# Two changes to a planned kernel: K of the first chunk placed by ScalarE in layer 1 too, and engine orders drawn up again on a model of the port that VectorE and GpSimd share

## The chip, the cores and the metric

The kernel runs on one core of a Trainium2 chip. The core has five engines that run side by side[...]: TensorE (PE, matmuls; its weight loads are listed as PEld), VectorE (DVE), ScalarE (ACT), GpSimd (POOL) and SyncE (SP, which here only starts DMA transfers). TensorE writes into PSUM, which has eight banks of 512 f32 per partition; the other data lie in SBUF. The metric is the device time of one execution in microseconds, as a median over several executions. Beside it there is one profiled execution, from which every duration below is taken.

## The reference

Two layers with the same weights; each is a windowed attention block and a token-mixing MLP, with layer normalisations and residuals. The input is 2048 tokens of 512 features, bf16; there are 32 heads of 16 features and a window of 256 tokens; the MLP has 1792 hidden units over the token axis.

```python
def _A_ref(x, wqkv, wo):
    H = 32; Dh = D // H; W = 256
    q, k, v = ...                      # x @ wqkv, split in heads
    scores = einsum("bhqd,bhkd->bhqk", q, k) * (Dh ** -0.5)
    mask = (idx[:, None] - idx[None, :] >= 0) & (idx[:, None] - idx[None, :] < W)
    p = softmax(where(mask, scores, -1e9), axis=-1)
    return einsum("bhqk,bhkd->bhqd", p, v)...reshape(B, S, D) @ wo

def _B_ref(x, w1, b1, w2, b2):
    h = layernorm(x)
    u = gelu(einsum("bsd,sf->bdf", h, w1) + b1)
    return (einsum("bdf,fs->bds", u, w2) + b2).transpose(0, 2, 1)

for layer in range(2):
    x = x + _A_ref(layernorm(x), A_wqkv, A_wo)
    x = x + _B_ref(layernorm(x), B_w1, B_b1, B_w2, B_b2)
```

## The kernel before

**Tiling.** The 2048 tokens are four chunks (m = 0 to 3) of four tiles of 128. For each chunk `prepare` normalises the tiles, `qkv` transposes them on TensorE (L750) and projects K, Q (L767) and V (L797); `attention` runs over four groups o of eight heads; `wo_block` projects back and adds the residual (L968, L972); `u_part` adds the chunk's share of the MLP's first matmul to a running sum (L1014, L1023, L1026); `y_block` does the second matmul (L1037, L1042). The y blocks of layer 0 run within layer 1's `prepare`, so that layer 1's attention has MLP matmuls of layer 0 to fill TensorE with, and its own u parts later.

**Attention of one group.** The scores (L851) need K laid out as a block-diagonal `kbd`, in which the even and the odd heads (h = 0, 1) have their own half and zeros elsewhere. ScalarE takes the exponential of two PSUM banks at a time (L863), VectorE multiplies the probabilities `pt` in place by a 0/1 mask from `ldm` (L876 for one cell, L879 for two or more), TensorE multiplies by V (L896), VectorE copies the two results into `cs` (L940), DMAs bring the sums together (L946 to L954 and after) and back as `md` by way of DRAM, and GpSimd multiplies `cs` by `md` into `oT` (L958), which `wo_block` reads.

**How K comes into `kbd`.** The projection leaves K of one group in a PSUM bank. As a rule VectorE (L734) or in some chunks ScalarE (L736) casts it into a bf16 buffer `stg`, and GpSimd writes the two halves of `kbd` from it, each with a 0/1 column of `par` as multiplier (L783). For the groups listed in `KACT`, as (layer, chunk, group), ScalarE writes both halves straight from PSUM with `par` as its scale (L776), and `stg` isn't used. Before, `KACT` holds the four groups of chunk 0 in layer 0.

**Where the order comes from.** Every operation is an entry in a `Graph` with an engine, a cost, the data that it reads and writes, and a priority. `schedule` simulates the five engines: at each step `_pick` chooses for an engine the operation that could start first, with rules for scores, PV matmuls and a priority number; `RANK` shifts the priority of each dense group of matmuls by hand. The outcome is one fixed order of instructions per engine. `reorder` then moves single entries of that order by the offsets in `MOVES` (one tuple each for TensorE, VectorE, ScalarE, GpSimd and SyncE). `emit` writes the instructions out in this order with the semaphore waits that the data need. So each engine runs a fixed list, and an instruction that waits holds up all behind it on its engine, transfers on SyncE's queue included. The costs and simulated times only shape the order; none of them is in the program that runs.

**The port in the planner.** `ported` holds two times, until when VectorE's and until when GpSimd's port operations last. Before, an operation of VectorE counts if it is marked `port` (only the normalisation L700 is), and every operation of GpSimd counts:

```python
            if e == "vector" and o.port:
                t = max(t, self.ported[1])
            elif e == "gpsimd":
                t = max(t, self.ported[0])
...
                if e == "gpsimd" or e == "vector" and o.port:
                    self.ported[e == "gpsimd"] = o.end
```

The masks L876 and L879 are not marked.

Of the kernel before, what the change touches and what calls it, by code (L numbers as in the profile page):

```python
# [21 lines left out]
    -18, 0, -107, -93, 7, 6, -38, -55, -48, 11, -12, 10, 37, -42, 7, 0, -4, -7, 17, -3, -66, 62, -49, 16, 1, 15,  # L22
    -19, 14, -4, 0, 6, 0, -51, 35, 0, 0, 0, 15, -56, -10, 52, 0, -146, 0, -473, -256, 101, -200, 193, 399, 0, 49,
    -23, 0, -1, 18, 8, 17, -12, 11, -1, -10, -4, 7, 6, -31, -47, -15, 10, 0, 0, 15, -362, 42, 322, -14, -380, 0,
    -24, 312, 0, 0, -17, -8, -15, 0, 5, -20, 0, 11, 0, 0, 142, 93, 62, -58, 23, 2, 27, -54, -6, 41, 164, 28, -29,
    -57, 31, 0, 1, -46, 60, 13, 0, -18, 28, -176, 115, -122, 460, -486, -53, 10, -5, 0, 0, 0, 0, 0, -39, -32, -78,
    0, -2, 0, 0, 0, 0, 0, -52, 0, 0, 0, 0, 0, 0, 0, 19, -6, -6, -13, -155, -126, 144, -106, -33, -173, 6, -9, 0,
    -137, 0, 5, -40, 152, 260, 0, -12, 4, 14, -8, 17, -14, 0, 16, -188, 4, 8, 15, -2, 4, -8, 0, 0, -65, 0, 1, 9, -2,
    -112, 11, 0, -15, -114, 0, 7, 3, 4, -12, 10, -16, 0, 9, 6, 12, 0, -28, 0, 0, 117, 31, -17, -17, 0, 0, 473, 47,
    0, -9, -3, -9, -384, -150, -479, 217, 122, 0, 36, 157, 53, 18, -27, 0, -6, 0, -120, 0, 1, 50, 52, 12, 14, 193,  # L30
    -18, 13, 0, 0, 0, 113, 408, -134, 107, -30, -22, -52, 0, 14, -17, 0, 0, 186, -153, -439, 359, -146, 0, -3, 15,
    -10, 13, 10, -109, 5, 157, -86, -10, -52, -43, 17, -46, -58, -33, -135, -167, -266, 232, 53, -3, 56, -33, -31,
    -16, 104, -18, -39, 0, 0, 3, 0, -1, 0, 0, 0, 0, 0, 0, 0, 0, 0, 0, 0, 0, 0, 0, 0, 0, 0, 0, 0, 0, 0, 0, 6,
# [3 lines left out]
        5, 5, -1, 0, 3, 8, -4, 2, -8, 2, -6, 1, -4, 1, -4, 0, 0, 0, 0, 1, 1, -2, 0, 0, 0, 0, 0, 0, 0, 2, -1, -1, 0,  # L37
        0, 0, 0, 0, 0, 0, 0, 1, 3, -2, -1, -1, 0, 0, 1, -1, 0, 0, 0, 0, 0, 0, 0, 1, -1, 0, 0, 0, 0, 0, 0, 0, 0, 0,
        0, 0, 0, 0, 0, 0, 0, 0, 0, 0, 0, 1, -1, 0, 1, -1, 0, 0, 0, 0, 0, 0, 0, 0, 0, 0, 0, 0, 0, 0, 0, 0, 0, 0, 0,
        1, -1, 0, 0, 0, 0, 0, 0, 0, 0, 0, 0, 0, 0, 0, 0, 0, 0, 0, 0, 0, 0, 0, 0, 0, 0, 0, 0, 0, 0, 0, 0, 0, 0, 0, 0,  # L40
        0, 0, 0, 0, 0, 0, 0, 0, 0, 0, 0, 0, 0, 0, 0, 0, 0, 0, 0, 0, 0, 0, 0, 0, 0, 0, 0, 0, 0, 0, 0, 0, 0, 0, 0, 0,
        0, 0, 0, 1, -1, 0, 0, 0, 0, 0, 0, 0, 0, 0, 0, 0, 0, 0, 0, 0, 0, 0, 1, -1, 2, -1, -1, 2, -1, -1, 0, 0, 0, 0,
        0, 0, 0, 0, 0, 0, 0, 0, 0, 0, 0, 0, 0, 0, 0, 0, 0, 0, 0, 0, 0, 0, 0, 0, 0, 6, -1, -1, -1, -1, -1, -1, 0, 1,
        -1, 1, 1, -2, 0, 1, 4, 0, -3, 2, 2, 2, -4, 1, -5, 0, 1, -1, 0, 0, 0, 0, 0, 0, 8, 1, 1, 1, -4, -4, -1, 2, -2,
        -2, 0, 0, 0, 0, 22, 22, 22, -3, -3, 7, 7, 18, 10, 5, 9, 9, 9, -11, -11, -11, -10, -10, -3, -3, -12, -16,
        -13, -6, -14, 1, 1, -16, 0, 0, 0, 0, 0, 0, 0, 0, 0, 0, 0, 0, 0, 0, 0, 0, 0, 0, 0, 0, 0, 0, 0, 0, 0, 0, 0, 0,
        0, 0, 1, -1, 0, 0, 0, 1, 1, -2, 0, 1, -1, 1, 1, -2, 0, 0, 0, 0, 0, 0, 0, 0, 0, 0, 0, 0, 0, 0, 0, 0, 0, 0, 0,
        0, 0, 0, 0, 0, 0, 0, 0, 0, 0, 0, 0, 0, 0, 0, 0, 0, 0, 0, 0, 0, 0, 0, 0, 0, 1, -1, 0, 0, 0, 0, 0, 0, 0, 0, 0,
        0, 0, 1, -1, 0, 0, 3, -1, 0, -2, 0, 4, -1, -1, -1, -1, 3, -1, -1, -1, 0, 0, 0, 0, 0, 0, 0, 0, 0, 0, 0, 0, 0,
        0, 0, 0, 0, 0, 0, 0, 0, 0, 0, 0, 0, 1, -1, 0, 0, 0, 0, 0, 0, 0, 0, 0, 0, 0, 0, 0, 0, 0, 1, -1, 0, 1, -1, 1,  # L50
        -1, 0, 0, 0, 0, 0, 0, 0, 0, 0, 0, 0, 0, 0, 0, 0, 1, -1, 0, 0, 0, 0, 0, 0, 1, -1, 0, 0, 0, 0, 0, 0, 0, 0, 0,
        0, 0, 0, 0, 0, 0, 0, 0, 0, 0, 0, 0, 0, 0, 0, 0, 0, 0, 0, 0, 0, 2, 0, 1, -3, 0, 0, 0, 0, 0, 0, 0, 0, 0, 0, 0,
        0, 0, 1, -1, 0, 0, 0, 0, 0, 0, 0, 0, 0, 0, 0, 0, 0, 0, 0, 0, 0, 0, 0, 0, 0, 0, 0, 0, 0, 0, 0, 0, 0, 0, 0, 0,
        1, -1, 0, 1, -1, 2, -1, -1, 1, -1, 0, 0, 1, -1, 0, 0, 2, 2, 2, -3, 2, -4, -1, 0, 0, 0, 1, 1, 1, 1, -4, 0, 0,
        2, 2, 2, -3, 1, -4, 0, 0, 0, 0, 0, 0, 0, 0, 0, 3, -1, 2, 2, -3, -3, 21, -1, 3, 14, 18, 1, 1, -6, 1, -7, 3,
        14, -9, 1, -4, -7, 13, -2, -2, -15, -9, -9, -4, 3, 9, 5, 5, -8, -5, 8, 4, -11, -5, -9, 11, 3, -4, 4, 4, -11,
        6, -6, -3, 6, -1, -5, 1, -3, 5, 5, -14, 6, -2, -2, -6, 0, 5, 5, -6, -3, 3, 4, -4, -4, 0, 4, 4, -7, -2, 2, 7,
        2, 0, -6, 0, 0, 0, -9, 0, 0, 0,
    ),
    (  # L60
        6, -1, 3, 8, 8, 8, 8, 9, 7, 9, 9, 6, 8, 8, -7, -7, 6, 6, 11, -10, 5, -17, 15, 3, 3, 9, -16, 22, 5, -1, 5,
        -7, -31, -2, 2, 18, 12, 13, -8, -37, 1, -3, -3, 0, -4, 2, -4, 24, -4, -3, 4, -19, -1, 13, 1, -3, 9, 1, -13,
        -3, 4, 2, -5, -1, 16, -5, 9, 1, -1, 0, 2, 2, 2, 8, 2, -16, -15, 5, 9, 6, 4, 2, 4, 5, 5, 5, 5, 6, 4, 5, 5, 5,
        -22, -15, 4, 5, 1, 4, 5, 5, -1, 5, 3, 5, 3, 4, -4, -30, -29, 1, 2, 0, 1, 2, 0, 1, 1, 3, 0, 3, 3, 0, 2, 2, 2,
        2, 2, 2, -9, 1, 1, 1, 1, 1, 1, 1, 1, 1, 2, 0, 1, 1, 3, 1, 2, 3, 1, 2, 3, -6, 0, 2, 2, 2, -2, 4, 0, 1, -1, 2,
        0, 1, 1, 3, 1, 2, 2, 8, 1, -5, 2, 3, 5, -2, 4, 1, 3, 7, -5, -9, 3, 1, -1, 2, -4, 2, 3, -1, 2, 2, -2, 1, 1,
        1, -191, 0, 0, 0, 0, 0, 0, 0, 0, 1, -1, 0, 0, 2, -1, 1, 1, -3, 0, 0, 0, 0, 1, -1, 0, 0, 0, 1, -1, 0, 0, 0,
        0, 2, 0, 2, 0, 2, -5, -1, 1, 1, 2, 2, -1, 2, 0, 2, 0, 1, 1, 2, 6, 2, 0, -15, 1, -1, 2, 3, -1, -9, 2, 0, 2,
        0, -5, 1, -1, 1, 1, 1, 2, -4, -1, 1, 2, 0, 1, 1, -5, 0, 0, 3, 0, 0, -3, 0, 0, 0, 0, 1, -1, 0, 0, 0, 0, 0, 0,
        1, 1, 3, 1, 2, 2, 2, 2, -8, 2, 2, 2, 2, -10, 1, 1, 1, -7, 0, 0, 0, 2, 0, 2, 0, -4, 0, 0, 1, 1, -2, 1, -1, 1,  # L70
        -1, 0, 0, 0, 0, 0, 4, -1, -1, -1, -1, 0, 0, 2, 0, 5, 3, 0, 0, -6, 3, 3, 0, 2, -8, 1, 1, -6, 0, 0, 0, 0, 3,
        1, -1, -3, 5, 1, 2, -3, -1, -4, 0, 0, 0, 0, 0, 0, 0, 0, 0, 0, 1, -1, 0, 0, 0, 0, 1, 1, 1, 1, -4, 0, 0, 0, 0,
        0, 2, 2, 2, 6, -4, 1, -1, 6, 7, -1, 0, -4, -1, -12, 2, 2, -4, 1, 1, -5, 0, 0, 0, 2, -1, -1, 0, 2, 2, 2, -2,
        2, 2, 3, -2, 4, 2, 3, -11, 4, 1, 1, 4, 4, 1, -10, -2, 2, 2, 2, 2, -14, 1, 2, 2, 4, -2, 0, -10, 4, -2, 4, 2,
        4, 2, 3, 3, -7, -7, 2, 2, 3, 3, 0, 2, -5, 3, 0, 2, -1, 1, -19, 0, 0, 3, 0, 0, -3, 0, 1, -1, 0, 0, 4, 1, 3,
        4, -3, 1, 2, -4, 1, 1, 1, 1, 1, 1, 1, 1, 1, 1, -18, 4, -1, 1, -1, 1, -4, 1, 2, -2, 1, 3, 1, 2, 2, -3, 2, 0,
        3, 1, 3, 1, 3, 3, 3, 8, 6, -3, 10, -10, 12, -2, -4, 1, 11, 4, -5, 7, 9, -30, 9, -11, -2, 5, 7, -2, 0, 3, 6,
        3, -13, -10, 4, 2, -1, -19, -21, 0, 0, 0, 1, 1, 1, 1, 1, 1, 1, 1, -8, 0, 0, 0, 0, 0, 0, 0, 0, 0, 0, 2, 0,
        -2, 0, 1, -1, 0, 0, 1, 1, 1, 1, 1, 1, 1, 3, 0, 2, 3, 4, 0, 3, 0, 2, 2, -17, -9, 1, 2, 0, -3, 2, -1, 1, 1, 2,
        2, -1, -6, 1, 1, 1, -3, 0, 1, -1, 0, 1, 1, -2, 0, 1, 1, 2, 4, 2, -5, -1, 1, -5, 1, -1, 2, 0, 1, 4, 1, -5, 3,  # L80
        3, -4, -1, 2, -5, 1, 1, -3, 3, 0, 2, -1, 1, 2, 3, 5, 5, 5, -4, 4, 4, 4, 4, 4, -8, 3, 3, 3, -10, -10, 1, -23,
        0, 0, 0, 3, 0, -2, 1, 4, -3, 0, 0, 1, 2, 3, 1, -7, 3, 5, 8, -1, 4, -4, -2, -10, -1, 2, 4, -6, 1, 2, -5, -3,
        0, 1, 2, -2, -1, 1, -1, 0, 0, 0, 2, 0, -2, 1, 2, -2, -1, 1, 1, 1, -3, 3, -1, 0, -2, 2, 0, -2, 0,
    ),
    (
        0, 0, 0, 0, 1, -1, 0, 0, 0, 1, -1, 0, 0, 0, 0, 0, 0, 0, 0, 0, 0, 0, 0, 0, 0, 0, 0, 0, 0, 0, 0, 0, 0, 0, 0,
        0, 0, 0, 0, 0, 0, 0, 0, 0, 0, 0, 0, 0, 0, 0, 0, 0, 0, 0, 0, 0, 0, 0, 0, 0, 1, -1, 0, 0, 0, 0, 0, 1, -1, 0,
        0, 0, 0, 0, 0, 0, 0, 0, 0, 0, 0, 0, 0, 0, 0, 1, -1, 0, 0, 0, 0, 0, 0, 0, 0, 0, 0, 0, 0, 0, 1, -1, 0, 0, 0,
# [35 lines left out]
KACT = {(0, 0, o) for o in range(4)}  # L124
# [31 lines left out]
class Graph:  # L156
# [108 lines left out]
    def _pick(self, e, cand, ready, free, mode):  # L265
# [8 lines left out]
        for o in cand:  # L274
            t = free
# [5 lines left out]
            elif e == "gpsimd":  # L281
                t = max(t, self.ported[0])
# [831 lines left out]
```

## Time and profile before

| | |
|---|---|
| median of 5 runs | 482.51 us (480.79 to 485.57) |
| profiled execution, its own time | 483.6 us |
| its span, first to last instruction | 481.9 us |
| mean granted TensorE clock | 0.996 |

Groups of instructions that the change concerns, from the profile:

| line, engine | what | count | mean of one |
|---|---|---|---|
| L863 ACT | exponential, 2 banks | 288 | 1037 ns |
| L734 DVE | cast of K to `stg` | 24 | 679 ns |
| L736 ACT | cast of K to `stg` | 4 | 595 ns |
| L783 POOL | half of `kbd` from `stg` | 56 | 779 ns |
| L879 DVE | mask, 1024 elements | 72 | 755 ns |
| L876 DVE | mask, 512 elements | 72 | 498 ns |
| L958 POOL | `oT` = `cs` x `md` | 30 | 1366 ns |
| L696 POOL | power of the normalisation, 2 columns | 24 | 764 ns |

Read the views so: busy time tells how long an engine worked, not whether anyone waited for it. The chain of work that ended last is followed back from the last instruction, at each step to what released it, so an instruction on it did set the end in this execution. A timeline line gives start, duration, engine, source line, operation, operands and count; in brackets stands the idle time before it and what ended that. Neighbouring VectorE instructions overlap a little in the record: a cast listed with 0.68 us is followed by the next after 0.60.

### The profile page before, as it was taken

Reading aid. Unit: us, or ns where it says so; the run is one execution under the profiler, and the core shown is the slowest. Engines: PE = TensorE matmul, PEld = TensorE weight load, DVE = VectorE, ACT = ScalarE, POOL = GpSimd, SP = SyncE. Lnnn points to the kernel's source line nnn. Section 1 sums busy time; section 2 is a strip of 40 time slices with the busy share of each in tenths; the row PEclk is TensorE's granted clock in tenths of the full one; section 3 lists DMA queues with packets and bytes.
Section 4 is the critical chain, followed back from the end, with each engine's and each line's share of the span. In section 5 each row is a group of like instructions: output and inputs, shape, how many; then the busy total and the mean of one; then the engine's idle time right before and its main releaser. Section 6 shows DMA issues by size and latency. Waiting matters only on the chain.

```text
span 481.9 us, 15719 instructions
## 1 busy us (share of the span) xinstructions
PE 436.8 (91%) x6831; PEld 208.7 (43%) x6831; DVE 370.2 (77%) x747; ACT 323.5 (67%) x367; POOL 133.6 (28%) x205
## 2 busy tenths in 40 slices
PE   7988887797888789999999989997989989999997
PEld 4454443353333344455344444443534434444443
DVE  6989989787988979765797698789995986942332
ACT  2889999998988970623898889787868982052000
POOL 3243442343414313025012532443184121200000
PEclk9989999999999999999999999999999999999999
DMA  8403431224153333231044333120415356434564
GB/s 237 146 1 97 113 107 32 57 79 116 41 162 88 109 118 111 66 104 51 12 127 119 92 101 92 53 70 28 121 32 147 100 159 185 119 89 122 164 177 160
DMA packets 83993, 49.47 MB, mean 103 GB/s; under 512 B 14676, under 2 KB 78164, under 8 KB 83924
## 3 DMA queue, kind: packets, MB, share of 16 engines
q1 hardware_dynamic: 83924, 48.46, 35.3%
q8 instruction: 54, 0.88, 0.8%
q14 instruction: 15, 0.12, 0.1%
HBM read 41.43 MB, written 2.59 MB: 91 GB/s over the span
## 4 chain that ended last, share of the span: by engine, by line
PE 60%; DVE 17%; ACT 16%; POOL 3%; issue 2%; DMA 1%; SPq 1%; POOLq 0%
PE PS L1037 17%; PE PS L1014 16%; ACT pt L863 14%; PE PS L767 6%; PE PS L851 5%; PE PS L797 5%; PE PS L896 5%; PE PS L968 3%; DVE pt L876 3%; DVE cs L940 2%; DVE pt L879 2%; POOL kbd L783 2%; DVE qT L734 1%; DVE stats L689 1%; PE PS L616 1%
## 5 line engine op out<-in xcount | busy, mean ns | idle before, releaser
L863 ACT ACTIVATE pt<-PS 128x1024 bf16<-128x1024 f32 (+1 forms) x304 | 284.3, 1026 | 42.9 <-PE PS L851 39.9
L1014 PE MATMUL PS<-xh_sb,w1b 128*128 128x512 bf16 x448 | 106.2, 380 | 3.6 <-ACT pt L863 1.8
L1037 PE MATMUL PS<-ub,w2b 128*128 128x512 bf16 x448 | 103.3, 380 | 0.1
L851 PE MATMUL PS<-qT,kbd 32*128 32x64 bf16 (+4 forms) x1632 | 61.1, 244 | 21.9 <-ACT pt L863 7.4
L767 PE MATMUL PS<-xhT,wqkv 128*128 128x512 bf16 x256 | 63.8, 384 | 1.9 <-ACT pt L863 1.4
L958 POOL TENSOR_TENSOR oT<-cs,md 128x512 bf16<-128x512 f32 x30 | 40.9, 1366 | 87.5 <-DMA cs<-cs 47.4
L1014 PEld LDWEIGHTS PS<-xh_sb,w1b 128*128 128x128 bf16 x448 | 40.1, 98 | 57.0 <-issue 5.7
L1037 PEld LDWEIGHTS PS<-ub,w2b 128*128 128x128 bf16 x448 | 41.5, 98 | 50.6 <-issue 3.7
L783 POOL TENSOR_SCALAR kbd<-stg,par 128x512 bf16<-128x512 bf16 x56 | 43.2, 779 | 60.7 <-DVE stg L734 37.7
L879 DVE TENSOR_TENSOR pt<-pt,ldm 128x1024 bf16<-128x1024 bf16 (+1 forms) x80 | 56.9, 721 | 3.2 <-ACT pt L863 3.1
L1026 DVE TENSOR_TENSOR ub<-PS,ub 128x512 f32<-128x512 f32 x70 | 45.3, 684 | 15.6 <-PE PS L1014 15.4
L851 PEld LDWEIGHTS PS<-qT,kbd 32*128 32x128 bf16 x1632 | 23.5, 92 | 75.3 <-ACT pt L863 40.4
L1042 DVE SCALAR_TENSOR_TENSOR x_sb<-PS,bcol,x_sb 128x512 bf16<-128x512 f32 x32 | 23.4, 746 | 41.6 <-PE PS L1037 41.5
L940 DVE COPY cs<-PS 128x512 f32<-128x512 f32 x60 | 38.6, 683 | 14.1 <-PE PS L896 13.8
L1029 ACT ACTIVATE ub<-ub,bcol 128x512 bf16<-128x512 f32 x28 | 18.3, 712 | 43.7 <-DVE ub L1026 43.6
L876 DVE TENSOR_TENSOR pt<-pt,ldm 128x512 bf16<-128x512 bf16 (+1 forms) x104 | 43.6, 440 | 2.2 <-ACT pt L863 1.8
L896 PE MATMUL PS<-pt,vt 64*18 64x64 bf16 (+4 forms) x3040 | 39.0, 242 | 6.4 <-DVE pt L876 1.8
L694 POOL TENSOR_SCALAR rstd<-agg 128x2 f32<-128x2 f32 (+1 forms) x40 | 8.9, 222 | 125.4 <-DVE agg L691 124.3
L689 DVE BATCH_NORM_STATS2 stats<-x_sb 128x6 f32<-128x512 bf16 x64 | 42.7, 681 | 0.9 <-DMA x_sb<-in_A_x_dram 0.6
L896 PEld LDWEIGHTS PS<-pt,vt 64*18 64x18 bf16 x3040 | 30.7, 84 | 15.8 <-ACT pt L863 3.6
L797 PE MATMUL PS<-wqkv,xhT 128*64 128x256 bf16 x512 | 33.7, 277 | 2.3 <-DVE cs L940 0.8
L767 PEld LDWEIGHTS PS<-xhT,wqkv 128*128 128x128 bf16 x256 | 22.1, 98 | 30.2 <-issue 3.2
(54 smaller groups left out, 324.8 us busy)
## 6 DMA issues: line engine op xcount, KB each, us to landing
w2b<-in_B_w_dram SPq DMA_DIRECT2D x112, 128.0 KB, 2.6
w1b<-in_B_w_dram SPq DMA_DIRECT2D x56, 256.0 KB, 3.4
md<-rscr SPq DMA_DIRECT2D x30, 256.0 KB
cs<-cs SPq DMA_DIRECT2D x120, 32.0 KB, 2.9
out_dram<-x_sb SPq DMA_DIRECT2D x16, 128.0 KB, 3.0
x_sb<-in_A_x_dram SPq DMA_DIRECT2D x3, 512.0 KB
wqkv<-in_A_wqkv_dram SPq DMA_DIRECT2D x2, 384.0 KB, 7.5
x_sb<-in_A_x_dram SPq DMA_DIRECT2D x4, 128.0 KB, 2.1
```

The source lines that it names most:

```text
L689: op("vector", lambda e, t=t: e.bn_stats(stats[:, t, :], x_sb[:, t, :]), reads=[f"x{t}"], writes=[f"st{t}"], cost=dve_cost(512))
L767: mm_group(ft, 4, lambda e, c: e.matmul(PS[:, ft.slot, :], lhsT=wqkv[:, c, which * 512 + o * P:which * 512 + (o + 1) * P], rhs=xhT[:, tx.s ...
L783: op("gpsimd", lambda e, h=h: e.tensor_scalar(kbd[:, tk[o].slot, :, h, :], stg[:, ts.slot, :].rearrange("p (s n) -> p s n", n=64), par[:, ...
L797: last = e.matmul(PS[64 * hf:64 * hf + 64, ft.slot, sc * 256:(sc + 1) * 256], lhsT=xhT[:, tx.slot, c, tok:tok + 64], rhs=wqkv[:, c, 1024:1 ...
L851: last = e.matmul(PS[:, bank(r), c0 * 64:(c0 + nb) * 64], lhsT=kbd[32 * r:32 * r + 32, tkk.slot, jj, :, :].rearrange("p h n -> p (h n)"), ...
L863: return e.activation(pt[:, tp.slot, 2 * u:2 * u + 2, 0:n], PS[:, b0:b0 + 2, 0:n], ACTF.Exp, scale=SMSCALE)
L876: return e.tensor_tensor(v, v, msk.unsqueeze(1).to_broadcast([P, 4, w]), op=ALU.mult)
L879: return e.tensor_tensor(v, v, msk.unsqueeze(1).unsqueeze(1).to_broadcast([P, 4, k, w]), op=ALU.mult)
L896: last = e.matmul(PS[32 * r:32 * r + 18, tO[h].slot, q0 * 64:(q0 + nb) * 64], lhsT=vt[64 * h:64 * h + 64, tvv.slot, jj, 4 * o + r, :], rhs ...
L940: op("vector", lambda e, tO=tO[h], tc=tc, h=h: e.tensor_copy(cs[:, tc.slot, h], PS[:, tO.slot, :]), reads=[tO[h]], writes=[(tc, h)], cost= ...
L1014: out_ = e.matmul(PS[:, tu.slot, :], lhsT=w1b[:, tw.slot, s, tt * P:(tt + 1) * P], rhs=xh_sb[:, 4 * m + s, :], start=(n == 0 and s == 0), ...
L1037: mm_group(ft, NFT, lambda e, fc: e.matmul(PS[:, ft.slot, :], lhsT=w2b[:, tws[fc // W2F].slot, fc % W2F, k * P:(k + 1) * P], rhs=uT(fc), s ...
```

## The change

`KACT` takes in chunk 0 of layer 1. In the planner, masks are marked `port`, and so are the long GpSimd operations (L783, the V placements L813, L958); GpSimd's other operations, the two of each normalisation (L694, L696) among them, no longer count. Two windows of `_pick` for layer 0 are 250 and 50 ns in place of 300 and 0. `RANK` and all five tuples of `MOVES` are new: the order of every engine is another. Of the instructions that run, only those for K of chunk 0 in layer 1 are of another kind.

```diff
 RANK = (
...
 MOVES = (
...
-KACT = {(0, 0, o) for o in range(4)}
+KACT = {(l, 0, o) for o in range(4) for l in range(2)}
...
-            if e == "vector" and o.port:
-                t = max(t, self.ported[1])
-            elif e == "gpsimd":
-                t = max(t, self.ported[0])
+            if o.port:
+                t = max(t, self.ported[e == "vector"])
...
-    WINDOW = ({0: 400.0, 1: 300.0, 2: 0.0}, {0: 150.0, 1: 400.0, 2: 400.0})
+    WINDOW = ({0: 400.0, 1: 250.0, 2: 50.0}, {0: 150.0, 1: 400.0, 2: 400.0})
...
-                if e == "gpsimd" or e == "vector" and o.port:
+                if o.port:
                     self.ported[e == "gpsimd"] = o.end
...
-                       reads=[ts, ("par", h)], writes=[(tk[o], h)], cost=pool_cost(512, 1))
+                       reads=[ts, ("par", h)], writes=[(tk[o], h)], cost=pool_cost(512, 1), port=True)
...
-                           writes=[("vb", v0, h)], cost=pool_cost(128, 1))
+                           writes=[("vb", v0, h)], cost=pool_cost(128, 1), port=True)
...
-                        op("vector", f_mask, reads=keys + LD, writes=keys, cost=dve_cost(4 * len(cells) * w, 0.5), tag="mask")
+                        op("vector", f_mask, reads=keys + LD, writes=keys, cost=dve_cost(4 * len(cells) * w, 0.5), tag="mask",
+                           port=True)
...
-                   reads=[(tc, 0), tm] + [(tc, "up", r) for r in range(4)], writes=[to], cost=1400)
+                   reads=[(tc, 0), tm] + [(tc, "up", r) for r in range(4)], writes=[to], cost=1400, port=True)
```

## The prediction

> **What bounds the kernel now.** I read the page's busy row first, then the busy time by stage, then the chain of work that ended last, then the timelines of single engines where the chain pointed. The page, in which each entry is busy time, share of the span and instructions:
>
> ```profile
> span 481.9 us, 15719 instructions
> ...
> PE 436.8 (91%) x6831; PEld 208.7 (43%) x6831; DVE 370.2 (77%) x747; ACT 323.5 (67%) x367; POOL 133.6 (28%) x205
> ```
>
> TensorE is busy in all but 45.1 us (481.9 - 436.8). The change adds and removes no matmul, so what it gains or loses has to appear in those 45.1 us. The stages show where they lie (stretch, its length, then busy time and instructions of each engine):
>
> ```profile
> core 0: us, PE busy (x) PEld busy (x) DVE busy (x) ACT busy (x) POOL busy (x), PEclk, DMA share, GB/s
> 0.00:20.00 20.00, 17.15 (x139) 8.98 (x140) 14.85 (x46) 9.67 (x15) 7.51 (x27) 1.00 0.69 205
> 20.00:180.00 160.00, 135.64 (x2963) 66.47 (x2961) 140.10 (x286) 143.96 (x160) 54.23 (x70) 0.99 0.31 88
> 180.00:244.00 64.00, 63.41 (x489) 29.15 (x491) 46.86 (x95) 28.15 (x37) 13.88 (x27) 1.00 0.25 72
> 244.00:400.00 156.00, 142.19 (x2884) 69.12 (x2880) 130.90 (x260) 130.62 (x142) 53.79 (x72) 1.00 0.35 97
> 400.00:481.90 81.90, 78.44 (x381) 35.01 (x368) 37.45 (x63) 11.08 (x16) 4.16 (x9) 1.00 0.48 142
> ```
>
> TensorE idles 24.4 us in the attention of layer 0 (20 to 180), 13.8 us in that of layer 1 (244 to 400), and next to nothing from 180 to 244, where matmuls of the MLP fill every gap. So 38.2 us can be won, all in the two attention stages. There ScalarE is at 90% and 84%, VectorE at 88% and 84%: three engines pass the limit to and fro. The chain agrees: 60% TensorE, 17% VectorE, 16% ScalarE, 3% GpSimd. Its pieces (start, length, what) include masks far longer than their work:
>
> ```profile
> 280.17 1.60 DVE pt L879
> ...
> 300.00 3.76 POOL kbd L783 x4
> ...
> 396.66 1.35 DVE pt L876
> ```
>
> The L879 mask of 1024 elements usually takes 0.68 us, the L876 mask of 512 takes 0.41. GpSimd's timeline shows what ran beside two of these, and VectorE's timeline shows the same two masks:
>
> ```profile
> 279.95 2.94 POOL L958 TENSOR_TENSOR oT<-cs,md 128x512 bf16<-128x512 f32 x2 [3.34 <-issue]
> ...
> 396.45 1.26 POOL L958 TENSOR_TENSOR oT<-cs,md 128x512 bf16<-128x512 f32 x1
> ```
>
> ```profile
> 280.09 1.68 DVE L879 TENSOR_TENSOR pt<-pt,ldm 128x1024 bf16<-128x1024 bf16 x1
> ...
> 396.58 1.42 DVE L876 TENSOR_TENSOR pt<-pt,ldm 128x512 bf16<-128x512 bf16 x1
> ```
>
> The mask at 396.58 starts 0.13 us behind a GpSimd multiply that ends at 397.71 and itself ends at 398.00, some 0.3 behind it: it stood still for about 1.0 us. This is the collision that the new planner knows of and the old one did not.
>
> **Part 1: K of chunk 0 in layer 1.** It removes four casts to `stg` and eight GpSimd placements, and adds eight ScalarE placements. Layer 0 has these already, so their price is in the trace:
>
> ```profile
> L776 ACT ACTIVATE kbd<-PS,par 128x512 bf16<-128x512 f32 x8 | 5.2, 717 | 0.0
> ```
>
> On the chain a pair of them takes 1.16 to 1.24 us; four pairs are 4.6 us of ScalarE. Removed are 4 x 0.60 = 2.4 us of VectorE (the pace of its casts) and 8 x 0.69 = 5.5 us of GpSimd; the stage in which they lie has 17 us of VectorE idle and most of GpSimd, so I value both at nothing. A placed K would be ready sooner: now the first cast starts at 220.81 and its first halves are placed from 221.61, some 2.2 us for a pair; then 1.2. Whether that starts the exponentials sooner depends on TensorE's order. TensorE, then ScalarE, at this place:
>
> ```profile
> 219.75 5.34 PE L767 MATMUL PS<-xhT,wqkv 128*128 128x512 bf16 x24
> 225.02 0.40 PE L851 MATMUL PS<-qT,kbd 32*128 32x320 bf16 x8
> ```
>
> ```profile
> 217.62 0.59 ACT L736 CAST vt<-PS 128x512 bf16<-128x512 f32 x1
> 225.47 1.94 ACT L863 ACTIVATE pt<-PS 128x1024 bf16<-128x1024 f32 x2 [7.26 <-PE PS L851]
> ```
>
> Six projections run in a row before the first score, and ScalarE waits 7.26 us for it. With a new order the first K is projected at 220.8, placed at 222.1, and the first exponential could start near 222.8, 2.7 us sooner. One pair lies in the 7.26 us for nothing; the other three (3.5 us) stand among the exponentials, and whatever is queued behind them on ScalarE waits, with the scores that need those PSUM banks behind that. Ends: 2.7 us won (the three pairs lie in ScalarE's waits, which from 225.5 to 241.4 sum to 2.4 us) and 4.6 us lost (first score no sooner, every pair in the way). I take 3.5 - 2.7 = 0.8 us lost. The cover that could make it nothing is that TensorE has MLP matmuls to run until 244.
>
> **Part 2: the new orders.** All five engines' orders change, SyncE's too, so no single move can be priced. The trace does show what the model change is aimed at. I went through the chain and took from each collided piece its usual duration:
> - starts that a DMA set, because the GpSimd multiply had waited for `cs` or `md`: masks at 143.00 (0.42), 144.95 (1.07), 174.18 (0.90), 260.42 (0.59), 325.32 (1.05), 327.78 (0.77): 4.8 us;
> - starts that the order set: 124.42 (placements and the power behind them, 0.69), 257.60 (0.38), 280.09 (1.00), 300.00 (four placements at 0.94 in place of 0.67: 1.07), 353.57 (0.82), 396.58 (1.00): 5.0 us.
>
> In all 9.8 us of the chain. Off the chain is as much again: L879 72 x (755 - 682) = 5.3 us, L876 72 x (498 - 411) = 6.3 us, and GpSimd's own, 56 x (779 - 696) + 30 x (1366 - 1273) = 7.4 us, 19 us in all. An order can keep a mask from a placement that is queued by hand, but where a transfer's landing starts the multiply, a plan that mistakes the landing by half a microsecond is no help. So I take the second group, 5.0 us, and leave the first. Ends: 9.8 us won (both groups) and, since the reordering also moves transfers past each other on SyncE and could put anything late, about as much lost as one more long wait costs; the nearest row is ScalarE's waits for scores (39.9 us in 55 waits, 0.7 each), so a handful, 3 us, lost.
>
> Behind a mask that is no longer late stands the next input of the same PV matmul or score: ScalarE's exponentials, 14% of the chain. With ScalarE at 84 to 90% in these stages, more than about half of the chain's collisions cannot be cashed without meeting it; that too is why I stop at 5.0.
>
> One rule speaks against the new model. It counts only GpSimd's long operations as users of the shared port; the small ones of the layernorm (L694, L696) are freed. The rows: L696 takes 0.69 us for two columns as a rule, but 1.23 at 127.48 while a mask ran from 127.48 to 128.17, and 1.17 at 317.52. The Trainium skill, "SBUF — State Buffer", section "SBUF: two separate sides", says that the port pair is an exclusive lock which the first to start keeps for its whole instruction, and that it counts against any GpSimd operation that reads SBUF. By the rule each of the 40 small ones may stop a mask for 0.69 us; by the rows they are those that stop, by 0.5, and the normalisation behind them waits (3.4 us over 5 waits in this profile). By the model they cost nothing. If four more of them lay behind masks on the chain, that would be 2 us lost; I take none, as the old orders did not avoid them either.
>
> **Sum.** 0.8 - 5.0 = -4.2 us. The profiled execution took 483.6 us (span 481.9 and 1.7 around it), 1.1 above the median of 482.51; it would become 479.4, and the median 478.3, 0.9% less.
>
> **Rivals.**
> - *Nothing is won.* The masks are freed, but the exponentials behind them are just as late, and new collisions replace old ones, since the multiplies start when transfers land. For it: six of the twelve places are of that kind, and ScalarE's share. Against it: VectorE itself holds 17% of the chain. Time: 482.5.
> - *ScalarE becomes the bound in layer 1: slower.* The four pairs lie in front of exponentials, and the first score comes no sooner. Price 4.6 us, in full where ScalarE has less than 3.5 us of waits between 225 and 244 and TensorE's filler ends before ScalarE has caught up. For it: those waits are 2.4 us up to 241. Against it: from 244 to 400 ScalarE idles 25.4 us, so that most can be made up. Time: 487.1.
> - *More is won.* Both groups go and the exponentials start 2.7 us sooner: 482.5 - 12.5 = 470.0.
>
> **How the numbers follow.** Forecast 0.53, nothing won 0.20, ScalarE bound 0.15, more won 0.12. Half a percent, 2.4 us, is about what a measurement of this kernel can tell from no change. Faster by over that: 0.65; within it: 0.20; slower by over it: 0.15. The forecast's own range is 475 to 480. The range for 8 in 10 runs from 471.5, most of the way to the best case, to 485.5, inside the ScalarE case.
>
> **What would show it.** TensorE's busy time stays at 436 to 438 while its idle time falls from 45 to about 41 us, the fall lying in 244 to 400 more than in 20 to 180. The 1024 mask's mean falls from 755 to below 720 ns, the 512 mask's from 498 to below 460. Sixteen ScalarE placements at 717 ns; GpSimd placements down from 56 to 48. First exponential of layer 1 about 2.7 us sooner against its stage's first score. It is wrong if the masks' means fall and the span doesn't (nothing won), or if ScalarE has no gap from 222 to 250 and scores wait on it more than now (slower).

## The result and the profile after

| | before | after |
|---|---|---|
| median | 482.82 us (79 runs) | 480.66 us (44 runs) |
| ratio | | 0.9956, 95% interval 0.9942 to 0.9971 |
| profiled execution, span | 481.9 us | 478.6 us |

The changed kernel is 0.44% faster (2.1 us). The forecast was 0.9% (4.2 us): the right way, half the size. The profiled executions differ by 3.3 us, more than the medians; single executions of one kernel differ by a few microseconds, so the sizes below come from the ratios and the profiles tell only where. The changed kernel's line numbers are three smaller (L879 is now L876, L876 is L873, L783 is L780, L776 is L773, L863 is L860).

The page of the changed kernel, and its chain by engine:

```profile
span 478.6 us, 15704 instructions
...
PE 435.9 (91%) x6830; PEld 207.4 (43%) x6830; DVE 366.6 (77%) x746; ACT 326.8 (68%) x372; POOL 127.1 (27%) x197
...
PE 61%; ACT 22%; DVE 8%; issue 3%; DMA 2%; SPq 2%; POOL 2%; POOLq 0%
```

TensorE's busy time stays, as it had to; its idle time falls from 45.1 to 42.7 us. VectorE's share of the chain falls from 17% to 8%, ScalarE's rises from 16% to 22%: ScalarE is now more often the one that is late. The same stages as before (the number in brackets behind each engine's busy time is instructions):

```profile
20.00:180.00 160.00, 136.37 (x2963) 65.91 (x2964) 139.84 (x287) 143.04 (x159) 55.14 (x75) 0.99 0.31 84
180.00:244.00 64.00, 63.45 (x571) 30.06 (x570) 44.77 (x96) 35.20 (x47) 7.96 (x21) 1.00 0.27 78
244.00:400.00 156.00, 145.19 (x2816) 69.16 (x2812) 129.97 (x260) 129.55 (x140) 54.06 (x71) 1.00 0.36 100
```

Between 180 and 244 ScalarE has 7 us more and GpSimd 6 less, and TensorE is as full as it was. TensorE's idle time falls where the forecast put it: from 13.8 to 10.8 us between 244 and 400, and only from 24.4 to 23.6 between 20 and 180. The masks, by form (count, then busy time and mean of one):

```profile
L876 DVE TENSOR_TENSOR pt<-pt,ldm 128x1024 bf16<-128x1024 bf16 x72 | 53.3, 756 | 1.3 <-ACT pt L860 1.2
L873 DVE TENSOR_TENSOR pt<-pt,ldm 128x512 bf16<-128x512 bf16 x72 | 31.6, 451 | 2.0 <-ACT pt L860 1.9
```

The 512 mask's mean fell from 498 to 451 ns, as forecast; the 1024 mask's, which was to fall below 720, did not move (755 before). Collided masks are still on the chain:

```profile
97.48 1.66 DVE pt L876
...
100.88 0.36 DVE pt L873
...
106.80 2.10 DVE pt L876 x2
...
359.60 2.28 DVE pt L876 x2
```

GpSimd's timeline shows the same partner as before at all four. Three of these multiplies were started by a transfer; only the first stood behind other work of GpSimd:

```profile
97.32 1.27 POOL L956 TENSOR_TENSOR oT<-cs,md 128x512 bf16<-128x512 f32 x1
...
100.52 1.27 POOL L956 TENSOR_TENSOR oT<-cs,md 128x512 bf16<-128x512 f32 x1 [0.22 <-DMA md<-rscr]
...
106.49 1.27 POOL L956 TENSOR_TENSOR oT<-cs,md 128x512 bf16<-128x512 f32 x1 [2.33 <-DMA md<-rscr]
...
360.00 1.33 POOL L956 TENSOR_TENSOR oT<-cs,md 128x512 bf16<-128x512 f32 x1 [3.86 <-DMA md<-rscr]
```

Last, K of chunk 0 in layer 1, TensorE and then ScalarE:

```profile
217.70 4.48 PE L764 MATMUL PS<-xhT,wqkv 128*128 128x512 bf16 x20
222.11 0.40 PE L848 MATMUL PS<-qT,kbd 32*128 32x320 bf16 x8
```

```profile
218.77 1.27 ACT L773 ACTIVATE kbd<-PS,par 128x512 bf16<-128x512 f32 x2 [2.23 <-PE PS L764]
220.49 1.27 ACT L773 ACTIVATE kbd<-PS,par 128x512 bf16<-128x512 f32 x2 [0.46 <-PE PS L764]
222.22 1.26 ACT L773 ACTIVATE kbd<-PS,par 128x512 bf16<-128x512 f32 x2 [0.46 <-PE PS L764]
223.37 1.94 ACT L860 ACTIVATE pt<-PS 128x1024 bf16<-128x1024 f32 x2
```

Five projections now run ahead of the first score, not six: the score starts 4.41 us behind the first projection (before: 5.27), 0.9 us sooner. Three pairs, not one, lie ahead of the first exponential. So that exponential starts 5.67 us behind the first projection, where it started 5.72 behind it before: the 2.7 us that I counted did not come.

**A measure of collisions.** For each mask and each normalisation (L700) I took its duration less the lower quartile of its form, wherever that was over 0.12 us, and called the sum of one profile VectorE's collision sum. It is 13.6 us before and 9.4 after. In before's profile 9.9 us of it stand beside the multiply, 3.4 beside placements of K and 0.3 beside a normalisation's power; after, 7.6 and 1.8 and none.

### The profile page after: what moved, and what is told of

It is laid out like the page before. It is cut to its first block, busy times and chain, and to the rows that moved or that the text cites. A ratio compares the mean times of both kernels' runs of the same rounds, so it can differ in the third digit from the quotient of the medians.

```text
span 478.6 us, 15704 instructions
## 1 busy us (share of the span) xinstructions
PE 435.9 (91%) x6830; PEld 207.4 (43%) x6830; DVE 366.6 (77%) x746; ACT 326.8 (68%) x372; POOL 127.1 (27%) x197
## 4 chain that ended last, share of the span: by engine, by line
PE 61%; ACT 22%; DVE 8%; issue 3%; DMA 2%; SPq 2%; POOL 2%; POOLq 0%
ACT pt L860 20%; PE PS L1035 17%; PE PS L1012 16%; PE PS L894 6%; PE PS L764 5%; PE PS L848 5%; PE PS L966 5%; PE PS L794 4%; DVE pt L876 2%; DVE cs L938 2%; DMA w1b<-in_B_w_dram 1%; ACT kbd L773 1%; SPq L992 1%; PE PS L613 1%; SPq L944 1%
## 5 line engine op out<-in xcount | busy, mean ns | idle before, releaser
L860 ACT ACTIVATE pt<-PS 128x1024 bf16<-128x1024 f32 (+1 forms) x304 | 283.8, 1028 | 35.7 <-PE PS L848 33.3
L1012 PE MATMUL PS<-xh_sb,w1b 128*128 128x512 bf16 x448 | 107.6, 382 | 3.9 <-DMA w1b<-in_B_w_dram 1.1
L764 PE MATMUL PS<-xhT,wqkv 128*128 128x512 bf16 x256 | 62.4, 381 | 1.5 <-DVE vt L731 0.9
L956 POOL TENSOR_TENSOR oT<-cs,md 128x512 bf16<-128x512 f32 x30 | 38.8, 1294 | 90.4 <-DMA cs<-cs 46.9
L876 DVE TENSOR_TENSOR pt<-pt,ldm 128x1024 bf16<-128x1024 bf16 (+1 forms) x80 | 56.6, 721 | 3.0 <-ACT pt L860 2.8
L780 POOL TENSOR_SCALAR kbd<-stg,par 128x512 bf16<-128x512 bf16 x48 | 38.0, 801 | 64.2 <-DVE stg L731 49.7
L873 DVE TENSOR_TENSOR pt<-pt,ldm 128x512 bf16<-128x512 bf16 (+1 forms) x104 | 39.2, 399 | 4.0 <-ACT pt L860 3.9
```

What stands on the lines that cost most here:

```text
L764: mm_group(ft, 4, lambda e, c: e.matmul(PS[:, ft.slot, :], lhsT=wqkv[:, c, which * 512 + o * P:which * 512 + (o + 1) * P], rhs=xhT[:, tx.s ...
L860: return e.activation(pt[:, tp.slot, 2 * u:2 * u + 2, 0:n], PS[:, b0:b0 + 2, 0:n], ACTF.Exp, scale=SMSCALE)
L873: return e.tensor_tensor(v, v, msk.unsqueeze(1).to_broadcast([P, 4, w]), op=ALU.mult)
L876: return e.tensor_tensor(v, v, msk.unsqueeze(1).unsqueeze(1).to_broadcast([P, 4, k, w]), op=ALU.mult)
L1012: out_ = e.matmul(PS[:, tu.slot, :], lhsT=w1b[:, tw.slot, s, tt * P:(tt + 1) * P], rhs=xh_sb[:, 4 * m + s, :], start=(n == 0 and s == 0), ...
```

## The experiments

For orders to be moved from one kernel to the other, the program was written again with every engine's order and every tile's buffer as lists: with before's lists it issues before's instructions in before's order, and with the new lists those of the changed kernel. Line numbers of these files are again others.

### What each part does alone, and each layer

```diff
 # k_alone: before's lists
-vector:  ... kc3 kc0 ... kc2 kc1 ...        (four casts)
-gpsimd:  ... kb30 kb00 kb31 kb01 kb21 kb10 kb11 kb20 ...
+scalar:  xhT xhT vt  kb30 kb31 kb00 kb01 kb20 kb21  exp exp vt  kb10 kb11  exp ...
 # orders_alone: the changed kernel's lists
-scalar:  ... the eight kb ...
+vector:  ... kc0 q kc3 q kc2 vt kc1 ...
+gpsimd:  ... kb00 kb01 kb30 kb31 kb20 kb21 kb10 kb11 ...
 # layer0_new: operations of layer 0 as in the new lists, of layer 1 as in the old; layer1_new: the reverse
```

> The kernel before, every engine in its old order, with K of chunk 0 in layer 1 placed by ScalarE: the four casts and eight GpSimd placements are taken out of their queues, and the eight ScalarE placements put in where the changed kernel has them (three pairs ahead of the first two exponentials, one pair behind them). My theory (the new orders win, by fewer masks that meet GpSimd; K is about neutral): 482.8 to 483.6 us, ratio 1.000 to 1.002. Rival 'K does it': 480.7 us, ratio 0.9956. Rival 'ScalarE bound in layer 1': 485 to 487.

> The changed kernel's orders with the K edit taken back: chunk 0 of layer 1 again has four VectorE casts and eight GpSimd placements, put in at the places where K's matmuls end; all else in the new order. My theory: the gain is the orders', 480.7 us or a little less, ratio 0.994 to 0.996. Rival 'K does it': 482.8 us, ratio 1.000.

> Layer 0's operations in the changed kernel's order, layer 1's in the old one, K as before. By the two profiles layer 0 ends 2.05 us sooner after the change (the run of 42 y matmuls starts at 201.88, before at 203.93): if that shift is carried to the end, 480.7 us, ratio 0.9955 to 0.996. By my prediction's view (most of the fall in layer 1): ratio 0.998. If layer 1 gives it back: 1.000.

> Layer 0's operations in the old order, layer 1's in the changed kernel's, K on ScalarE in both layers. By the two profiles 1.2 us of the 3.3 us lie behind 244 us: 481.6 us, ratio 0.997 to 0.998. By my prediction's view: ratio 0.994 to 0.996. If layer 1's new order wins nothing: 1.000.

Measured: k_alone 1.0081 (1.0042 to 1.0119), orders_alone 0.9939 (0.9918 to 0.9961), layer0_new 1.0117 (1.0079 to 1.0156), layer1_new 1.0078 (1.0046 to 1.0110).

The orders win alone what the change wins, so "K does it" falls. K alone cost 3.9 us (486.7), which my theory did not have. The rival "ScalarE bound" did (485 to 487), though not for its reason, as k_early below shows. TensorE's timeline of k_alone:

```profile
226.99 0.81 PE L620 MATMUL PS<-xhT,wqkv 128*128 128x512 bf16 x3 [2.05 <-ACT kbd L629]
```

The fourth pair stood on ScalarE behind two exponentials and a cast; until it had read its PSUM bank, a projection of TensorE that needed the bank waited 2.05 us, and everything behind it on TensorE too. The clock then cost as much again. Three stretches of 3.41 us around this place, the wait lying in the second (PEclk, third from the end, is the granted clock):

```profile
core 0: us, PE busy (x) PEld busy (x) DVE busy (x) ACT busy (x) POOL busy (x), PEclk, DMA share, GB/s
221.22:224.63 3.41, 3.41 (x46) 2.23 (x45) 0.53 (x1) 2.71 (x4) 0.00 (x0) 1.00 0.00 0
224.63:228.04 3.41, 1.36 (x21) 0.57 (x18) 0.89 (x2) 2.08 (x4) 0.00 (x0) 1.00 0.00 0
228.04:231.45 3.41, 3.41 (x18) 1.04 (x8) 1.18 (x2) 1.94 (x2) 0.00 (x0) 0.50 0.02 5
```

By my estimate 3.41 us at half the clock lose 1.7 us of TensorE's work; with the wait that makes 3.75 of the 3.9 us. In the other executions the clock is lower too: its mean is 0.9921 over k_alone's eight and 0.9965 over those of before measured beside them.

The two hybrids were meant to place the gain and didn't. Either half of the new orders beside the other half of the old is slower than both kernels. Their profiles show longer waits for single transfers than TensorE and VectorE have in before's or the changed kernel's profile, such as this of TensorE in layer0_new from 280 to 335:

```profile
PE PS L897 <- DMA w2b<-in_B_w_dram: 4.9, 1, 4.9
```

In layer1_new VectorE waits 4.5 us for the transfer of sums into `rr` between 300 and 320 (before: 0.8 us in the whole profile). Whether the seam between the lists makes these waits was not settled. One thing they did teach: ScalarE's load of a new function table, which follows its last activation of layer 0, starts at 206.43 in before's profile and at 205.39 in the changed kernel's, but at 204.09 and 203.07 in k_alone and layer1_new, which run layer 0 in the old order. (Before's profile has a stretch of 3.4 us at half the granted clock at 29 us; those two have none by then.) The "2.05 us sooner" on which I put layer0_new's number was a difference between two executions, not between two orders.

### Where K may stand

```diff
 # k_early, against k_alone
-scalar:  kb30 kb31 kb00 kb01 kb20 kb21  exp exp vt  kb10 kb11
+scalar:  kb30 kb31 kb00 kb01 kb20 kb21  kb10 kb11  exp exp vt
 # k_pe, against k_alone
-tensor:  K3 K0 Q1 Q0 K2 K1 score V V V V Q3 score Q2
+tensor:  K0 Q1 K3 Q0 K2 score V V V V Q2 K1 Q3 score
-scalar:  kb30 kb31 kb00 kb01 kb20 kb21  exp exp vt  kb10 kb11
+scalar:  kb00 kb01 kb31 kb30 kb21 kb20  exp exp  kb11 kb10  vt
```

> As k_alone (old orders, K of chunk 0 in layer 1 on ScalarE), with the fourth pair of placements also ahead of the first two exponentials. In k_alone TensorE waited 2.05 us at this place for a bank that ScalarE had not yet read, and its clock was halved for 3.4 us afterwards. If the wait is the cause: 483 to 484, ratio 1.000 to 1.003 (1.2 us more of ScalarE ahead of the exponentials remains). If ScalarE's extra 4.6 us are the cause in themselves: no better than k_alone, ratio 1.007 or more.

> As k_alone, with the 14 groups of matmuls at this place (K, Q and V of chunk 0, the first two scores) and ScalarE's placements in the changed kernel's order: the fourth K is projected behind V. If K's cost is set by the order around it: ratio 1.000 to 1.002. If it is ScalarE's load: 1.007.

Measured: k_early 1.0004 (0.9978 to 1.0030), k_pe 1.0122 (1.0075 to 1.0169). With all four pairs ahead of the exponentials K costs nothing that can be told, and the projection that waited in k_alone runs without a wait. The new order of this place, set among old neighbours, is the worst of the three: TensorE waits for ScalarE's placements twice. TensorE's lines, k_early's first, then k_pe's:

```profile
226.26 1.04 PE L620 MATMUL PS<-xhT,wqkv 128*128 128x512 bf16 x4
```

```profile
224.83 1.94 PE L655 MATMUL PS<-wqkv,xhT 128*64 128x256 bf16 x32 [1.03 <-ACT kbd L628]
...
229.96 1.04 PE L619 MATMUL PS<-xhT,wqkv 128*128 128x512 bf16 x4 [1.36 <-ACT kbd L628]
```

All three kernels give ScalarE the same work, so it is not ScalarE's load that costs but the order, by way of the bank. (In k_pe the two waits are 2.4 of 5.9 us; what makes the rest was not followed.) My expectation for k_pe was wrong in taking the new kernel's order of 14 groups to be good by itself.

### What the collisions are worth

```diff
 # np_before, np_after
-gpsimd: kbd half = stg * par;  vb = vt * half;  oT = cs * md
+gpsimd: memset(stg part), memset(kbd half);  memset(scr), memset(vb);  memset(md part), memset(oT)
 # np_mul_*: only the multiply, as memset(cs part), memset(md part), memset(oT); np_place_*: only the placements
```

> The kernel before, orders untouched, with nothing on GpSimd that reads SBUF except the two small operations of each normalisation: the placements of K and V and the multiply into oT are replaced by fills of the same length in time (about 0.69, 0.37 and 1.27 us), which read nothing. Attention's result is left out by this, the work of all other engines is not. If every collided microsecond of the chain is worth one (9.8 us counted in the prediction): 473 us. If half, because something else is as late: 478. If nothing: 482.8. The 1024 mask should then take 0.68 us everywhere.

> The changed kernel with the same replacement. Its chain holds 3.9 us of collisions. If they are worth one for one: 476.8; if half: 478.7. What the two of these runs tell together: if fewer collisions are what the new orders win, this run and np_before come within 1 us of each other (this one up to 1 us later, for K on ScalarE). If the orders win by something else, this one stays 2 to 3 us below np_before.

> The kernel before, orders untouched, with only the multiply into oT replaced by three fills of together 1.27 us, which read nothing; the placements stay. Attention's result is left out. In the profile of before, VectorE's collisions sum to 13.6 us, 9.9 of them with the multiply and 3.4 with the placements. If a collision's worth goes by these shares, the multiply has 0.73 of the 6.5 us that np_before won: 4.8 us, 478.0, ratio 0.990. If most of what np_before won came from the placements or from its multiply being 0.35 us short: ratio 0.996 or more.

> The changed kernel with the same replacement of the multiply alone. Its profile has 7.6 us of VectorE's collisions with the multiply (before: 9.9) and 1.8 with the placements (before: 3.4). By shares: 0.8 of the 5.1 us that np_after lies below the changed kernel, 4.1 us: 476.6, ratio to before 0.987. If the new orders had taken the multiply's collisions out and left the others: ratio 0.994 or more, next to the changed kernel's 0.9956.

> The kernel before, orders untouched, with only the placements of K and V replaced by fills of the same length; the multiply stays. What the placements stand in the way of: 3.4 of 13.6 us of VectorE's collisions, and their own (4.6 us for K, 3.7 for V). By the shares of VectorE: 1.7 us won, ratio 0.9965. If GpSimd's own delays count as much as VectorE's: 4 us, ratio 0.992.

> The changed kernel with the same replacement of the placements alone. By the shares of VectorE: 1.0 us below the changed kernel, ratio to before 0.9935. If GpSimd's own delays count as much: 0.989.

Measured: np_before 0.9865 (0.9821 to 0.9909), np_after 0.9851 (0.9815 to 0.9888), np_mul_before 0.9886 (0.9838 to 0.9935), np_mul_after 0.9898 (0.9866 to 0.9930), np_place_before 1.0008 (0.9970 to 1.0045), np_place_after 0.9884 (0.9850 to 0.9919). In np_before and np_after the fills for the multiply took 0.86 us from the first start to the last end, in np_mul 1.14, both less than the 1.27 meant; all of before's profile has only 0.4 us in which another engine waits for `oT`.

The masks of np_before, same orders as before:

```profile
L737 DVE TENSOR_TENSOR pt<-pt,ldm 128x1024 bf16<-128x1024 bf16 x72 | 48.2, 679 | 3.7 <-ACT pt L721 3.6
L734 DVE TENSOR_TENSOR pt<-pt,ldm 128x512 bf16<-128x512 bf16 x72 | 29.0, 412 | 1.6 <-ACT pt L721 1.5
```

Their means are the undisturbed 0.68 and 0.41 us, though GpSimd is still busy for 104.0 us (before: 133.6): a fill stops no mask, a multiply does. So a GpSimd instruction can hold VectorE up with no semaphore between them. (The Trainium skill's "SBUF — State Buffer", "SBUF: two separate sides", says so for vector operations with two SBUF inputs: they contend only with a GpSimd operation that reads SBUF.) A fill does stop the normalisation: all that is left of the collision sum in np_before (0.6 us) and np_after (1.5 us) is normalisations that ran beside fills. The longest, in np_after, took 1.13 us in place of 0.40; VectorE's line, then GpSimd's:

```profile
271.45 1.13 DVE L554 TENSOR_SCALAR xh_sb<-x_sb,agg,rstd 128x512 bf16<-128x512 bf16 x1
```

```profile
271.30 0.53 POOL L642 MEMSET kbd<- 128x512 bf16 x1
271.76 0.21 POOL L641 MEMSET stg<- 128x128 bf16 x1
271.91 0.53 POOL L642 MEMSET kbd<- 128x512 bf16 x1
```

All collisions of before are worth 6.5 us. Without them old and new orders come within 0.7 us of each other, np_after ahead. That is the sign asked for, that fewer collisions are what the new orders win, but a weak one: with six executions of each, anything from np_after 2.6 us ahead to 1.3 us behind agrees with them. The line below is the stronger sign. np_after lies 5.1 us below the changed kernel, whose chain holds only 3.9 us of collisions: what is off the chain in one profile counts too. The multiply alone carries 5.5 of the 6.5. Taking the placements away won nothing in the old orders: there the multiply's collisions were 12.3 us in place of 9.9, so in that profile most of what one partner gave back was lost to the other. In the new orders it won more than I gave it (3.5 us below the changed kernel), with the multiply's collisions at 3.7 in place of 7.6. Why they fell that far was not tested. (That GpSimd's own delays count as much as VectorE's would have made 0.992 in the old orders and 0.989 in the new; the old speak against it, the new do not.) Either way the time went with the sum.

### The length of the hold

```diff
-tensor_tensor(oT[:, to.slot, :], cs[:, tc.slot, 0, :], md[:, tm.slot, :], op=ALU.mult)
+for c in (0, 256):
+    tensor_tensor(oT[:, to.slot, c:c + 256], cs[:, tc.slot, 0, c:c + 256], md[:, tm.slot, c:c + 256], op=ALU.mult)
```

> The kernel before, orders untouched, with each multiply into oT as two multiplies of 256 columns. So far the kernels lie near a line: 475.5 us plus half of VectorE's collision sum (before 13.6, changed 9.4, np_mul_before 4.7, np_before 0.6 us). If the length of GpSimd's hold sets what a mask can lose, the 9.9 us with the multiply fall to about 5, the sum to 8.7: 479.9 us, ratio 0.9945. If a mask that finds a hold loses the same to two short ones as to a long one, or the second half is stopped by masks in turn and oT comes late: ratio 0.999 or more.

> The changed kernel with each multiply in two halves. By the line: collisions with the multiply from 7.6 to 3.8, the sum to 5.6: 478.3 us, ratio to before 0.991. If splitting wins nothing: 0.9956, as the changed kernel.

> orders_alone (new orders, K of chunk 0 in layer 1 by VectorE and GpSimd as before) with each multiply in two halves. Its sum was 8.3 us, 6.0 of them with the multiply; by the line 5.3 us: 478.1, ratio 0.9905. If K on ScalarE is worth 0.8 us against these orders, this is the fastest of all versions that compute everything.

Measured: split_before 0.9913 (0.9879 to 0.9946), split_after 0.9907 (0.9886 to 0.9928), split_orders 0.9928 (0.9904 to 0.9953). The multiply and the masks of split_before:

```profile
L818 POOL TENSOR_TENSOR oT<-cs,md 128x256 bf16<-128x256 f32 x60 | 46.9, 803 | 81.8 <-DMA cs<-cs 42.6 <-DMA md<-rscr 39.0
L738 DVE TENSOR_TENSOR pt<-pt,ldm 128x1024 bf16<-128x1024 bf16 x72 | 51.4, 724 | 2.9 <-ACT pt L722 2.9
L735 DVE TENSOR_TENSOR pt<-pt,ldm 128x512 bf16<-128x512 bf16 x72 | 30.7, 436 | 1.4 <-ACT pt L722 1.2
```

A half takes 0.73 us by its median, so GpSimd works longer in all (46.9 us against 40.9), and still the kernel is 4.2 us faster with every instruction in its old place: about twice what the whole change won. The collisions with the multiply fell from 9.9 to 4.0 us. split_orders came out 1.0 us behind split_after and not ahead of it as expected; the intervals overlap.

**All runs on one line.** A straight line through the thirteen runs in which only collisions or K changed (ratio times 482.8 us against the collision sum of the profile) gives 475.2 us + 0.58 x sum, with a correlation of 0.97; no run is over 1.2 us off it. A like line (475.5 us and half of the sum) was on record before the three split runs; with the sums that these then had it gives 478.8 us for split_before, 478.0 for split_after and 479.1 for split_orders (measured 478.6, 478.3, 479.3).

| run | collision sum, us | ratio x 482.8 | by the line |
|---|---|---|---|
| before | 13.6 | 482.8 | 483.1 |
| k_early | 12.8 | 483.0 | 482.6 |
| np_place_before | 12.6 | 483.2 | 482.5 |
| changed kernel | 9.4 | 480.7 | 480.7 |
| orders_alone | 8.3 | 479.9 | 480.0 |
| split_orders | 7.1 | 479.3 | 479.3 |
| split_before | 6.6 | 478.6 | 479.0 |
| np_place_after | 5.0 | 477.2 | 478.1 |
| split_after | 5.0 | 478.3 | 478.1 |
| np_mul_before | 4.8 | 477.3 | 478.0 |
| np_mul_after | 2.5 | 477.9 | 476.7 |
| np_after | 1.5 | 475.6 | 476.1 |
| np_before | 0.6 | 476.3 | 475.6 |

k_alone (sum 13.9), k_pe (13.1), layer0_new (12.4) and layer1_new (8.0) lie 3.4 to 6.7 us above it, with the bank and the transfers named above. One profile stands for each run, so a sum is one sample.

The table also answers what np_before and np_after left open. A line through the six runs in the old order alone (before, k_early, np_place_before, split_before, np_mul_before, np_before) is 475.2 us + 0.58 x sum as well. It gives 480.7 us for the changed kernel and 480.1 for orders_alone (measured 480.7 and 479.9), so the new orders win what their smaller sum is worth, and no other gain is seen. Whether the port in the planner made the sum smaller, or the moves and ranks set by hand, was not tested.

## Why the prediction was half right

**What bounds the kernel** held: TensorE's work stayed, and the time moved with its idle time. That collided masks were what held VectorE up on the chain is shown by np_before, whose chain has 5% of VectorE in place of 17% (and 24% of ScalarE in place of 16%).

**Part 1, K.** I took 0.8 us lost. k_early says 0.2 (1.1 won to 1.4 lost); within the new orders, the changed kernel against orders_alone says 0.8 lost, split_after against split_orders 1.0 won, both within their intervals. K is worth nothing that was measured, and the sign stays open. The reasons that I gave were off: the first score comes 0.9 us sooner and the first exponential 0.05, not 2.7. And I named the banks in passing but priced only ScalarE's time; the 2.05 us that TensorE waits for a bank in k_alone are the larger danger.

**Part 2, the orders: here is the step that failed.** "So I take the second group, 5.0 us, and leave the first." Two things were in it, an amount and a price.

*How much is removed* was near. I split the chain's collisions into starts that a transfer set and starts that the order set, and let the second kind go. The new orders take 4.2 us (the changed kernel) or 5.3 us (orders_alone) out of VectorE's sum; on the chain, where I had counted 5.0 of 9.8 us, 3.9 are left in the changed kernel. The split was sound, too. The four masks of the second group lost 3.2 us in before's profile; the same masks lose 3.1 in k_early's, 3.0 in k_pe's and 1.8 in k_alone's. The six of the first group lost 4.8 us, and 1.1, 1.5 and 1.4 there: where a transfer starts the multiply, the place moves from profile to profile, while the sum stays (12.8 to 13.9 us in these four). And three of the four that are left on the changed kernel's chain are of the first kind.

*What a removed microsecond is worth* is what failed. I counted one for one, because each stood on the chain. It is 0.58 by the line. By the chain it has no fixed price: 0.66 by np_before (6.5 of 9.8 us), 1.3 by np_after (5.1 of 3.9 us). This is the term that was mis-sized: 4.2 to 5.3 us at 0.58 are 2.4 to 3.1 us, where 2.1 was measured for the whole change and 2.9 for the orders alone. I even wrote that more than half of the chain's collisions could not be cashed without meeting ScalarE, and used that as a reason to stop at 5.0, not to halve it. The chain of the changed kernel agrees with such a meeting: ScalarE's share is up by 6 points while VectorE's falls by 9. That ScalarE is why the price is 0.58 was not tested by itself.

**The rivals.** "Nothing is won" was right by about half in its mechanism. The 2.1 us lie inside the 2.4 that the prediction allowed to it, but the interval (1.4 to 2.8 us won) excludes no change. "ScalarE becomes the bound" didn't come: ScalarE took 3.3 us more and TensorE stayed full to 244. That the small operations of the normalisation are freed in the model cost little: of VectorE's collisions one of 24 was with them before (0.3 us), none after; it is mostly they that stop, as the prediction read from its rows.

What the new orders left is more than they took: np_after is 5.1 us below the changed kernel.

## What to carry to other kernels

A collided instruction on the chain is not worth its delay: ask what is next late. Here, where three engines share the limit, a microsecond of VectorE's collision sum, on the chain or off it, was worth about 0.6. Where a transfer starts GpSimd's operation, an order can't keep a mask from it for sure; make the hold shorter first (here two multiplies of 0.73 us for one of 1.27 won 4.2 us), then plan. When evacuation moves to another engine, price the PSUM bank that stays occupied, not only that engine's time (here 2.05 us of TensorE's wait and some 1.7 of half clock behind it).

## What was not expected of the hardware

The record of the granted clock has stretches of 3.4 us at half speed in 15 of the 17 profiles, one to three in each, and their places differ between runs of nearly the same order (29 us into the span before, 228 in k_alone, 84 and 354 in k_early, none inside layer1_new's span until its end). TensorE is then half as fast: four 512-column matmuls took 1.88 us in k_alone at 229.75, where four take 1.04.

The traces tell what comes before them: a stretch of the same 3.41 us in which TensorE was busy for 58% of the time or less. It was busy for 1.36 us of it in k_alone (224.63 to 228.04), 1.99 of 3.42 before (25.18 to 28.60), 1.44 and 1.53 in k_early. Cut into such stretches, the 15 profiles have 12 in which TensorE was busy for less than 43%, and all 12 are followed by half speed; of those between 43 and 58.5%, 11 are and 45 are not; of the 2021 above that, none is. So a wait of TensorE of 2 us can cost nearly twice its length. It is also much of the spread: over 324 executions, each taken against the mean of its kernel's executions measured together, the time rises by about 1.4 us where the mean granted clock falls by 0.0035, which is one such stretch (correlation -0.74). Part of what fewer collisions win comes this way, and the 0.58 holds it: the mean clock of split_after's executions is 0.9980, of before's beside them 0.9936.
